# Load order, Ln/Exp order and the place of a q turn at the start of a fused attention and FFN kernel

## The chip, the cores and the metric

The kernel runs on one core of one Trainium2 chip. The metric is device time in microseconds (us) of that core, as the median over executions of the whole kernel. Lower is better. Beside the timed runs there is one execution taken by the hardware profiler; all views quoted below come from it.

## The reference

Two computations follow each other: an attention whose keys and values are first projected from 1024 positions to 64, and a feed-forward layer with three parallel first matrices.

```
k_proj = E @ k ; v_proj = F @ v                 # per batch and head: 1024 -> 64 positions
scores = scale * q @ k_proj.T                   # 1024 x 64
attn   = softmax(scores)                        # max is taken off first, 1e-9 added to the sum
x      = attn @ v_proj                          # heads side by side: 8192 tokens x 512
h      = max(x @ w1, x @ w2, x @ w3)            # 512 -> 768, elementwise maximum of three products
out    = h @ w_out                              # 768 -> 512, float32
```

There are 8 batches of 8 heads, 1024 positions and 64 channels. All inputs are float32 in memory; the kernel works in bf16 with float32 accumulation.

## The kernel before

**Order of work.** The order of every instruction is written out by hand; no scheduler moves anything. Each engine works through its own list in the order in which the program emits it, and waits on semaphores where data, buffers or banks are not ready. The FFN of batch b is the trunk. For each of its two halves (chunks of 512 tokens) the function `l1` runs 18 times: for each of six column blocks jt, once for each of w1, w2 and w3 (i = 0, 1, 2). Each call is four matmuls into one of four rotating PSUM banks (0 to 3). The bank of w1 is copied out by ScalarE into `h1s` (L181), that of w2 is joined with `h1s` by VectorE into `m12` (L183), that of w3 with `m12` into `hT` (L185). `down` (L202, six matmuls over the six blocks of `hT`, copied out by ScalarE at L204) makes the output rows of a quarter chunk; every second one starts a store on POOL's queue (L209).

**Slots.** Between these calls the attention of batch b+1 is slipped in. After each `l1` or `down` a counter `slot` goes up by one in `tick`, and when it reaches the number that stands with a group, that group is emitted. The groups are `kv` (both projections, L117 and L119, then the copies to `kp2` at L123 and L124 and the turn of `kp2` into `kpT`, L166), `scores(0)` and `scores(1)` (four heads each, L136, with the Exp at L139), `sums` (the softmax sums by matmuls with ones, then on ScalarE Ln and Exp for each half u, L153 and L154, which give `rinv` = 1/sum), `av(0)` and `av(1)` (L146, each scaled by `rinv` on VectorE into `xT`, L159). All of them share PSUM banks 4 to 7, so each has to wait until the one before it has been read out.

During batch 0 the slots stand closer. Slots 1 to 12 belong to `l1_first` (L368), 13 to 16 to the first four `down`, 17 to 34 to the 18 calls of `l1` of the second chunk, 35 to 38 to its four `down`. Batch 1's attention sits there at slots 19 (`kv`), 26 and 29 (`scores`), 32 (`sums`), 34 and 36 (`av`); `q_pe1` at 22 and 24 turns batch 1's q on TensorE. From batch 1 on the slots are 2, 10, 15, 20, 25 and 30.

**Loads and turns.** Loads go through POOL's queue, at most eight outstanding in turn, and land in the order of issue. `load(b, ...)` issues two DMAs for q or k and three for v. `load_behind_turn(b)` first lets POOL copy one column of the `kpT` of the batch before (`seen`, L91), so that the loads of batch b are issued only after that turn has landed. q is turned by two transposing DMAs (`q_turn`, L97), one for four heads each, on SyncE's (SP) queue. The turn of `kp2` is on the same queue, so a turn that is emitted later runs behind it. In batch 0 both halves of batch 2's `q_turn` are emitted at slot 28; batch 2's `kv`, with its turn, comes at slot 2 of batch 1.

**Start.** Batch 0's attention runs ahead of everything, by pairs of heads: `k_proj0`, `scores0`, `v_proj0`, `av0`, `norm0`. The first chunk's product with w1 is `w1_ct(ct)` for four slices ct of the inner dimension (six matmuls each, L361). Slice 0 needs heads from the first two pairs alone, slices 2 and 3 need the last two pairs. `warmup` matmuls without use fill gaps.

Of the kernel before, what the change touches and what calls it, by code (L numbers as in the profile page):

```python
# [16 lines left out]
def kernel(ctx: ExitStack, tc: tile.TileContext, q, k, v, E, F, w1, w2, w3, w_out, out):  # L17
    nc = tc.nc
    B, H, S, D = q.shape
    KP = E.shape[0]  # L20
    P = 128
    SI = S // P
# [3 lines left out]
    NPAIR = H // 2  # L26
# [54 lines left out]
    def load(b, src, dst):  # L81
        sv = src[b].rearrange("h (p si) d -> p h si d", si=SI)
        parts = [(slice(0, 4), slice(0, 4)), (slice(4, 8), slice(4, 8))]
        if src is v:
            parts[1:] = [(slice(4, 8, 2), slice(5, 8, 2)), (slice(5, 8, 2), slice(4, 8, 2))]
        for slots, heads in parts:
            nc.gpsimd.dma_start(out=dst[b % NB][:, slots], in_=sv[:, heads])  # L87

    def load_behind_turn(b):

        nc.gpsimd.tensor_copy(out=seen, in_=kpT[(b - 1) % NB][:, 0, 0:1])  # L91
        load(b, q, q_t)
        load(b, k, k_t)
        load(b, v, v_t)

    def q_turn(b, hs):
        nc.sync.dma_start_transpose(  # L97
# [14 lines left out]
    def attention(b, turn):  # L112
        i = b % NB

        def kv():
            for si in range(SI):
                nc.tensor.matmul(out=ps[0:KP, AB, :], lhsT=eT[:, si, :], rhs=k_t[i][:, :, si, :],  # L117
                                 start=(si == 0), stop=(si == SI - 1))
                nc.tensor.matmul(out=ps[KP:P, AB, :], lhsT=fT[:, si, :], rhs=v_t[i][:, :, si, :],  # L119
                                 start=(si == 0), stop=(si == SI - 1))  # L120
            kv_k = ps[0:KP, AB, :].rearrange("p (h d) -> p h d", d=D)
            kv_v = ps[KP:P, AB, :].rearrange("p (g u dd f) -> p u g f dd", u=2, f=2, dd=HD)
            nc.scalar.copy(out=kp2[i][:, :, 0, :], in_=kv_k)  # L123
            nc.vector.tensor_copy(out=kp2[i][:, :, 1, :], in_=kv_k)  # L124
            turn(i)
            nc.scalar.copy(out=vp2[i][KP:P], in_=kv_v[:, 1])
            nc.vector.tensor_copy(out=vp2[i][0:KP], in_=kv_v[:, 0])

        def scores(u):
            for gg in range(2):  # L130
                g = 2 * u + gg
                for par in range(2):
                    r = slice(par * D, (par + 1) * D)
                    for col in range(2):
                        h = HEAD[2 * g + col]
                        nc.tensor.matmul(out=ps[col * KP:(col + 1) * KP, AB + 2 * gg + par, :],  # L136
                                         lhsT=kpT[i][r, h, :], rhs=qT[i][r, h, :, :], start=True, stop=True)
            for gg in range(2):
                nc.scalar.activation(out=pT[:, 2 * u + gg, :, :], in_=ps[:, AB + 2 * gg:AB + 2 * gg + 2, :],  # L139
                                     func=AF.Exp, scale=scale)  # L140

        def quads(lhs):
            for par in range(2):
                for hh, j, g, u in QUADS:
                    rows = slice(u * KP, (u + 1) * KP)
                    nc.tensor.matmul(out=ps[j * HD:(j + 1) * HD, AB + 2 * hh + par, :],  # L146
                                     lhsT=lhs(rows, g), rhs=pT[rows, g, par, :], start=True, stop=True,
                                     tile_position=(u * KP, j * HD))

        def sums():  # L150
            quads(lambda rows, g: ones[rows, :])
            for u in range(2):
                nc.scalar.activation(out=lns[u], in_=ps[:, AB + 2 * u:AB + 2 * u + 2, :], func=AF.Ln)  # L153
                nc.scalar.activation(out=rinv[u], in_=lns[u], func=AF.Exp, scale=-1.0)  # L154

        def av(half):
            quads(lambda rows, g: vp2[i][rows, g, half, :])
            for u in range(2):
                nc.vector.tensor_tensor(out=xT[b % 3][:, 2 * u + half, :, :], in0=ps[:, AB + 2 * u:AB + 2 * u + 2, :],  # L159
                                        in1=rinv[u].rearrange("p (c n) -> p c n", c=2), op=ALU.mult)  # L160

        return [(2, kv), (10, lambda: scores(0)), (15, lambda: scores(1)), (20, sums),
                (25, lambda: av(0)), (30, lambda: av(1))]

# [62 lines left out]
    def v_proj0(g, bank):  # L227
        for si in range(SI):
            for u in range(2):
                nc.tensor.matmul(out=ps[u * KP:(u + 1) * KP, bank, g * D:(g + 1) * D], lhsT=fT[:, si, :],  # L230
                                 rhs=v_t[0][:, HEAD[2 * g + u], si, :], start=(si == 0), stop=(si == SI - 1))
        nc.vector.tensor_copy(out=vp2[0][:, g], in_=ps[:, bank, g * D:(g + 1) * D].rearrange("p (dd f) -> p f dd", f=2))
# [54 lines left out]
    def warmup(n, bank):  # L287
        for _ in range(n):
            nc.tensor.matmul(out=ps[:, bank, :], lhsT=warm[:, 0:P], rhs=warm, start=True, stop=True)
# [8 lines left out]
        (nc.scalar if g % 2 else nc.sync).dma_start(out=q_st[:, 2 * g:2 * g + 2], in_=qv_[0][:, 2 * g:2 * g + 2])  # L298

    make_identity(nc, ident)  # L300
    for src, dst in ((k, k_t), (v, v_t)):
        sv = src[0].rearrange("h (p si) d -> p h si d", si=SI)
        for g in range(NPAIR):
            nc.gpsimd.dma_start(out=dst[0][:, 2 * g:2 * g + 2], in_=sv[:, 2 * g:2 * g + 2])
    wv = w1.rearrange("(hh r f) n -> hh f r n", hh=2, f=2)
    for ct in range(NCT):
        nc.gpsimd.dma_start(out=w_sb[0][:, ct, :], in_=wv[ct // 2, ct % 2])
    for wt, w in zip(w_sb[1:], (w2, w3)):
        for hh in range(2):
            nc.gpsimd.dma_start(out=wt[:, 2 * hh:2 * hh + 2, :],  # L310
                                in_=w[hh * 256:(hh + 1) * 256].rearrange("(r f) n -> r f n", f=2))
# [44 lines left out]

    W1B = (0, 1, 4, 5, 2, 3)

    def w1_ct(ct):
        for jt in range(NJT):  # L360
            nc.tensor.matmul(out=ps[:, W1B[jt], :], lhsT=w_sb[0][:, ct, jt * P:(jt + 1) * P], rhs=xT[0][:, ct, 0, :],  # L361
                             start=(ct == 0), stop=(ct == NCT - 1))

# [24 lines left out]
    av0(1, 0)  # L388
    norm0(0, 0, 6, (0,))
    norm0(0, 1, 7, (0,))  # L390
    for g in (2, 3):
        warmup(1, 2)
        v_proj0(g, 3)
    w1_ct(0)
    av0(0, 1)
    av0(1, 1)
    norm0(0, 0, 5, (1,))
    norm0(0, 1, 6, (1,))
    w1_ct(1)
    w1_ct(2)  # L400
    w1_ct(3)
    for jt in range(NJT):
# [3 lines left out]
    for b in range(B):  # L406
        groups = attention(b + 1, turn_dma) if b + 1 < B else []
        if b == 0:
            g1 = [g for _, g in groups]
            groups = [(10, q_up0), (11, scores_up0), (13, lambda: sums0(1, 4)), (15, av_up0),  # L410
                      (19, g1[0]), (22, lambda: q_pe1(0)), (24, lambda: q_pe1(1)), (26, g1[1]), (29, g1[2]),
                      (32, g1[3]), (34, g1[4]), (36, g1[5])]
        slot = 0
        gi = 0

        def tick():
            nonlocal slot, gi
            slot += 1
            while gi < len(groups) and groups[gi][0] <= slot:
                groups[gi][1]()  # L420
                gi += 1
            if b == 0:
                if slot == 22:
                    load_behind_turn(2)
                if slot == 28:
                    q_turn(2, slice(0, H // 2))
                    q_turn(2, slice(H // 2, H))
            elif b + 2 < B:
                if slot == 9:
                    load_behind_turn(b + 2)  # L430
                if slot == 18:
                    q_turn(b + 2, slice(0, H // 2))
                if slot == 27:
                    q_turn(b + 2, slice(H // 2, H))

        for ch in range(2):
            c = 2 * b + ch
            if c == 0:
                for i, jts, banks in ((1, range(6), (6, 7, 0, 1, 4, 5)), (2, range(3), (2, 3, 6)), (2, range(3, 6), (0, 1, 2))):
                    for _ in l1_first(i, jts, banks):  # L440
                        tick()
                state["f"] = 2
                for tt in range(4):
                    down(0, 0, 0, tt)
                    tick()
                continue
            for s in range(18):
                l1(b, ch, c, s // 3, s % 3)
                tick()
                if pend and s in (2, 5, 8, 11):  # L450
                    pend.pop(0)()
                    tick()
            pend = [lambda tt=tt, b=b, ch=ch, c=c: down(b, ch, c, tt) for tt in range(4)]
        if b == 0:
            while pend:
                pend.pop(0)()
                tick()
# [32 lines left out]
```

## Time and profile before

| | |
|---|---|
| median of 4 runs | 404.54 us (404.11 to 404.72) |
| the profiled execution's own time | 402.63 us |
| its span, first to last instruction | 400.8 us |
| TensorE busy | 392.2 us, 98% of the span |
| VectorE, ScalarE, POOL busy | 185.4, 167.7, 70.8 us |
| chain that ended last | 91% TensorE, 6% DMA, 1% ScalarE, 1% VectorE |

The span is the time from the first to the last instruction; 1.8 us more lie around it in the profiled execution. A busy TensorE is no TensorE at its peak, because its matmuls overlap and their ends are modelled: one matmul of 512 columns shows 379 ns, but 12 in a row take 2.70 us in the chain, about 0.22 us each. The chain is followed back from the last instruction to whatever released each step, so where it leaves TensorE, TensorE may have stood still for some or all of that piece.

### The profile page before, as it was taken

To read this page: it belongs to the slowest core of one execution; us is meant where nothing else is said; L and a number is where in the kernel's file an instruction comes from. 1 tells how busy PE (TensorE), PEld (TensorE's weight loads), DVE (VectorE), ACT (ScalarE), POOL (GpSimd) and SP (SyncE) were. 2 spreads that over 40 slices of the span, in tenths; PEclk is the share of its full clock that TensorE was granted. 3 is DMA by queue.
4 is the path that set the end of the run, shared out by engine and by line. 5 is a ranking of instruction groups with operands and counts; after the bars stand their busy time and mean duration, and the time that the engine had idled before them with its cause. 6 is when DMAs were issued, how large, how long until landed. Compare 5 with 4: busy or idle time off the path is not lost.

```text
span 400.8 us, 5985 instructions
## 1 busy us (share of the span) xinstructions
PE 392.2 (98%) x2422; PEld 170.9 (43%) x2422; DVE 185.4 (46%) x268; ACT 167.7 (42%) x248; POOL 70.8 (18%) x109
## 2 busy tenths in 40 slices
PE   7999999999999999999999999999999999999996
PEld 4444353434444444444444444444444444444443
DVE  3346354554653365533744246433655337433441
ACT  3413467346424553246322663245532473222222
POOL 7351150132001501051000500024010000000000
PEclk9899999999999999999999999999999999999999
DMA  9999969969951999149940899129991211102023
GB/s 227 206 209 206 213 162 194 206 107 189 201 119 52 174 170 195 56 94 184 227 138 13 155 192 232 52 59 171 192 170 57 63 52 50 56 0 106 1 104 107
DMA packets 62651, 53.73 MB, mean 134 GB/s; under 512 B 30496, under 2 KB 57632, under 8 KB 62624
## 3 DMA queue, kind: packets, MB, share of 16 engines
q0 software_dynamic: 31760, 43.52, 53.8%
q1 hardware_dynamic: 30032, 8.92, 15.4%
q10 hardware_dynamic: 832, 0.92, 0.7%
q8 instruction: 19, 0.31, 0.3%
q14 instruction: 8, 0.07, 0.1%
HBM read 57.15 MB, written 16.78 MB: 184 GB/s over the span
## 4 chain that ended last, share of the span: by engine, by line
PE 91%; DMA 6%; ACT 1%; DVE 1%; issue 0%; POOL 0%; POOLq 0%; DVEq 0%
PE ps L178 57%; PE ps L202 20%; PE ps L117 3%; PE ps L146 3%; DMA w_sb<-in_moe_w_dram 3%; PE ps L368 3%; PE ps L136 2%; DMA k_t<-in_k_dram 2%; DMA kpT<-kp 2%; PE ps L361 1%; ACT lns L153 0%; DVE xT L250 0%; PE ps L281 0%; PE ps L195 0%; PE ps L217 0%
## 5 line engine op out<-in xcount | busy, mean ns | idle before, releaser
L178 PE MATMUL ps<-xT,w_sb 128*128 128x512 bf16 x1080 | 246.6, 379 | 0.2 <-DVE xT L250 0.2
L178 PEld LDWEIGHTS <-w_sb 128*128 128x128 bf16 x1080 | 103.2, 98 | 132.7 <-issue 12.8
L183 DVE TENSOR_TENSOR m<-ps,h1s 128x512 f32<-128x512 f32 x90 | 62.1, 690 | 145.3 <-PE ps L178 114.9
L202 PE MATMUL ps<-wo_sb,hT 128*128 128x512 bf16 x378 | 91.2, 379 | 0.0
L181 ACT COPY h1s<-ps 128x512 f32<-128x512 f32 x90 | 52.6, 584 | 68.4 <-PE ps L178 68.0
L204 ACT COPY o_acc<-ps 128x512 f32<-128x512 f32 x63 | 36.8, 585 | 98.5 <-PE ps L202 98.5
L209 POOL DMA_DIRECT2D out_dram<-o_acc x30 | 21.2, 707 | 282.2 <-ACT o_acc L204 282.2
L185 DVE TENSOR_TENSOR hT<-ps,m 128x512 bf16<-128x512 f32 x90 | 62.3, 692 | 12.9 <-PE ps L178 4.8
L202 PEld LDWEIGHTS <-hT 128*128 128x128 bf16 x378 | 35.7, 98 | 47.2 <-issue 6.0
L159 DVE TENSOR_TENSOR xT<-ps,rinv 128x1024 bf16<-128x1024 f32 x28 | 32.9, 1217 | 8.5 <-PE ps L146 8.5
L139 ACT ACTIVATE pT<-ps 128x1024 bf16<-128x1024 f32 x28 | 27.2, 1022 | 12.4 <-PE ps L136 12.4
L87 POOL DMA_DIRECT2D v_t<-in_v_dram x21 | 15.3, 760 | 3.3 <-DMA w_sb<-in_moe_w_dram 3.3
L154 ACT ACTIVATE rinv<-lns 128x1024 f32<-128x1024 f32 x14 | 14.8, 1057 | 0.4
L153 ACT ACTIVATE lns<-ps 128x1024 f32<-128x1024 f32 x14 | 14.2, 1014 | 0.9 <-PE ps L146 0.9
L119 PE MATMUL ps<-v_t,fT 128*64 128x512 bf16 x56 | 13.4, 382 | 0.0
L117 PE MATMUL ps<-k_t,eT 128*64 128x512 bf16 x56 | 13.4, 382 | 0.0
L87 POOL DMA_DIRECT2D q_t<-in_q_dram x14 | 10.6, 764 | 4.4 <-DMA q_t<-in_q_dram 2.0
L368 PE MATMUL ps<-xT,w_sb 128*128 128x512 bf16 x48 | 10.9, 379 | 0.0
L123 ACT CAST kp<-ps 64x512 bf16<-64x512 f32 x7 | 4.0, 578 | 16.0 <-PE ps L119 16.0
L87 POOL DMA_DIRECT2D k_t<-in_k_dram x14 | 10.5, 765 | 0.8 <-issue 0.4
L124 DVE CAST kp<-ps 64x512 bf16<-64x512 f32 x7 | 4.8, 682 | 12.2 <-ACT kp L123 12.2
L146 PE MATMUL ps<-pT,vp 64*32 64x512 bf16 x224 | 9.1, 381 | 1.0 <-ACT lns L153 1.0
(77 smaller groups left out, 141.9 us busy)
## 6 DMA issues: line engine op xcount, KB each, us to landing
out_dram<-o_acc POOLq DMA_DIRECT2D x30, 512.0 KB, 5.1
q_t<-in_q_dram POOLq DMA_DIRECT2D x15, 512.0 KB, 7.8
k_t<-in_k_dram POOLq DMA_DIRECT2D x14, 512.0 KB, 13.0
v_t<-in_v_dram POOLq DMA_DIRECT2D x18, 256.0 KB, 17.7
v_t<-in_v_dram POOLq DMA_DIRECT2D x7, 512.0 KB, 16.7
w_sb<-in_moe_w_dram POOLq DMA_DIRECT2D x4, 384.0 KB, 10.3
k_t<-in_k_dram POOLq DMA_DIRECT2D x4, 256.0 KB, 7.9
w_sb<-in_moe_w_dram POOLq DMA_DIRECT2D x4, 192.0 KB, 10.2
```

The lines of the kernel that those rows point to most:

```text
L87: nc.gpsimd.dma_start(out=dst[b % NB][:, slots], in_=sv[:, heads])
L117: nc.tensor.matmul(out=ps[0:KP, AB, :], lhsT=eT[:, si, :], rhs=k_t[i][:, :, si, :], start=(si == 0), stop=(si == SI - 1))
L139: nc.scalar.activation(out=pT[:, 2 * u + gg, :, :], in_=ps[:, AB + 2 * gg:AB + 2 * gg + 2, :], func=AF.Exp, scale=scale)
L159: nc.vector.tensor_tensor(out=xT[b % 3][:, 2 * u + half, :, :], in0=ps[:, AB + 2 * u:AB + 2 * u + 2, :], in1=rinv[u].rearrange("p (c n) -> ...
L178: nc.tensor.matmul(out=ps[:, bank, :], lhsT=w_sb[i][:, ct, jt * P:(jt + 1) * P], rhs=xT[b % 3][:, ct, ch, :], start=(ct == 0), stop=(ct == ...
L181: nc.scalar.copy(out=h1s[jt % 2], in_=ps[:, bank, :])
L183: nc.vector.tensor_tensor(out=m12[jt % 2], in0=ps[:, bank, :], in1=h1s[jt % 2], op=ALU.max)
L185: nc.vector.tensor_tensor(out=hT[c % 2][:, jt, :], in0=ps[:, bank, :], in1=m12[jt % 2], op=ALU.max)
L202: nc.tensor.matmul(out=ps[:, bank, :], lhsT=hT[c % 2][:, jt, tt * P:(tt + 1) * P], rhs=wo_sb[:, jt, :], start=(jt == 0), stop=(jt == NJT - 1))
L204: nc.scalar.copy(out=o[:, tt, :], in_=ps[:, bank, :])
L209: nc.gpsimd.dma_start(out=dst[:, tt - 1:tt + 1, :], in_=o[:, tt - 1:tt + 1, :])
L368: nc.tensor.matmul(out=ps[:, bank, :], lhsT=w_sb[i][:, ct, jt * P:(jt + 1) * P], rhs=xT[0][:, ct, 0, :], start=(ct == 0), stop=(ct == NCT ...
```

## The change

The diff has four parts.

- **Start.** w1's slice 0 is loaded ahead of batch 0's last v pair instead of behind it. `w1_ct(0)` runs before the last `v_proj0`, which moves from bank 3 to bank 7; one half of `w1_ct(1)` runs ahead of the second `av0`, the other half behind. One `warmup` matmul goes.
- **`sums`.** Both Ln are emitted ahead of both Exp, in every batch.
- **Slots of batch 1's attention in batch 0.** `scores(0)`, `scores(1)` and `sums` come one slot earlier.
- **Batch 2.** It loads k, v, q instead of q, k, v. The first half of its `q_turn` stays at slot 28 of batch 0; the second goes to slot 3 of batch 1, behind the turn of batch 2's `kp2`.

```diff
-    def load_behind_turn(b):
+    def load_behind_turn(b, order="qkv"):
         nc.gpsimd.tensor_copy(out=seen, in_=kpT[(b - 1) % NB][:, 0, 0:1])
-        load(b, q, q_t)
-        load(b, k, k_t)
-        load(b, v, v_t)
+        for c in order:
+            load(b, *{"q": (q, q_t), "k": (k, k_t), "v": (v, v_t)}[c])
...
             for u in range(2):
                 nc.scalar.activation(out=lns[u], in_=ps[:, AB + 2 * u:AB + 2 * u + 2, :], func=AF.Ln)
+            for u in range(2):
                 nc.scalar.activation(out=rinv[u], in_=lns[u], func=AF.Exp, scale=-1.0)
...
+    for g in range(NPAIR):
+        load0(k, k_t, g)
+    for g in range(NPAIR - 1):
+        load0(v, v_t, g)
     for ct in range(NCT):
         nc.gpsimd.dma_start(out=w_sb[0][:, ct, :], in_=wv[ct // 2, ct % 2])
+        if ct == 0:
+            load0(v, v_t, NPAIR - 1)
...
-    for g in (2, 3):
-        warmup(1, 2)
-        v_proj0(g, 3)
+    v_proj0(2, 3)
+    warmup(1, 2)
     w1_ct(0)
+    v_proj0(3, 7)
+    w1_ct(1, range(3))
     av0(0, 1)
     av0(1, 1)
     norm0(0, 0, 5, (1,))
     norm0(0, 1, 6, (1,))
-    w1_ct(1)
+    w1_ct(1, range(3, NJT))
     w1_ct(2)
...
-                      (19, g1[0]), (22, lambda: q_pe1(0)), (24, lambda: q_pe1(1)), (26, g1[1]), (29, g1[2]),
-                      (32, g1[3]), (34, g1[4]), (36, g1[5])]
+                      (19, g1[0]), (22, lambda: q_pe1(0)), (24, lambda: q_pe1(1)), (25, g1[1]), (28, g1[2]),
+                      (31, g1[3]), (34, g1[4]), (36, g1[5])]
...
                 if slot == 22:
-                    load_behind_turn(2)
+                    load_behind_turn(2, "kvq")
                 if slot == 28:
                     q_turn(2, slice(0, H // 2))
-                    q_turn(2, slice(H // 2, H))
-            elif b + 2 < B:
+                return
+            if b == 1 and slot == 3:
+                q_turn(2, slice(H // 2, H))
+            if b + 2 < B:
```

More of the change, by code (lines that the diff above doesn't have):

```diff
@@ L300, with load0 @@
     make_identity(nc, ident)
[L301 to L304, printed above, removed]
     wv = w1.rearrange("(hh r f) n -> hh f r n", hh=2, f=2)
+    def load0(src, dst, g):
+        nc.gpsimd.dma_start(out=dst[0][:, 2 * g:2 * g + 2],
+                            in_=src[0].rearrange("h (p si) d -> p h si d", si=SI)[:, 2 * g:2 * g + 2])
+    for g in range(NPAIR):
+        load0(k, k_t, g)
+    for g in range(NPAIR - 1):
+        load0(v, v_t, g)
     for ct in range(NCT):
         nc.gpsimd.dma_start(out=w_sb[0][:, ct, :], in_=wv[ct // 2, ct % 2])
+        if ct == 0:
+            load0(v, v_t, NPAIR - 1)
     for wt, w in zip(w_sb[1:], (w2, w3)):
@@ L357, with w1_ct @@
     W1B = (0, 1, 4, 5, 2, 3)
-    def w1_ct(ct):
-        for jt in range(NJT):
+    def w1_ct(ct, jts=range(NJT)):
+        for jt in jts:
             nc.tensor.matmul(out=ps[:, W1B[jt], :], lhsT=w_sb[0][:, ct, jt * P:(jt + 1) * P], rhs=xT[0][:, ct, 0, :],
```

## The prediction, made before the changed kernel had run

> **What bounds the kernel now.** I read the page first (shares and chain), then the chain of waits in order of time, TensorE's own waits, the timeline where those waits lie, and the DMA queues by stretch. The page:
>
> ```profile
> PE 392.2 (98%) x2422; PEld 170.9 (43%) x2422; DVE 185.4 (46%) x268; ACT 167.7 (42%) x248; POOL 70.8 (18%) x109
> PE 91%; DMA 6%; ACT 1%; DVE 1%; issue 0%; POOL 0%; POOLq 0%; DVEq 0%
> ```
>
> TensorE sets the end. A change pays only where TensorE stands still, and costs wherever it makes TensorE stand still. The chain in order of time shows where it leaves TensorE:
>
> ```profile
> 8.91 10.70 DMA w_sb<-in_moe_w_dram
> ...
> 19.66 1.47 PE ps L361 x6
> ...
> 65.27 1.02 ACT lns L153
> ...
> 67.37 0.92 ACT lns L153
> ...
> 79.96 6.29 DMA kpT<-kp
> ...
> 86.29 0.63 PE ps L136 x8
> ```
>
> TensorE's waits say how much of these pieces is a real standstill:
>
> ```profile
> PE ps L146 <- ACT lns L153: 1.0, 1, 1.0
> ...
> PE ps L136 <- DMA kpT<-kp: 0.7, 1, 0.7
> ```
>
> So of the 6.29 us of the kpT turn only 0.7 are lost. The first wait is dearer than its 1.0: one L146 starts at 66.95 and the other fifteen at 68.33, 1.38 us lost. The timeline there shows ScalarE's queue:
>
> ```profile
> 64.67 0.58 ACT L181 COPY h1s<-ps 128x512 f32<-128x512 f32 x1 [0.77 <-PE ps L178]
> ...
> 65.26 1.02 ACT L153 ACTIVATE lns<-ps 128x1024 f32<-128x1024 f32 x1
> ...
> 68.31 1.06 ACT L154 ACTIVATE rinv<-lns 128x1024 f32<-128x1024 f32 x1
> ```
>
> Ln, Exp, Ln, Exp follow one another from 65.26 to 69.37, and the copy L181 stands ahead of them. Last, the DMA queues, packets, MB and share, for 66 to 74 us:
>
> ```profile
> q0 software_dynamic: 1246, 1.24, 91.1%
> q1 hardware_dynamic: 1248, 0.32, 30.1%
> ```
>
> and for 200 to 201 us:
>
> ```profile
> q1 hardware_dynamic: 1032, 0.26, 128.1%
> ```
>
> q0 carries the loads, q1 the turns. Beside loads a turn gets 1248/8 = 156 packets per us; alone up to 1032.
>
> **What the Trainium skill says.** "DMA: Bandwidth & Descriptors", Queues, rings and completion order: each DMA engine goes round its queues packet by packet. The 1246 against 1248 packets agree. "TensorE: Matmul & The Clock Gate", Part 1: after an idle window of about 3.4 us TensorE drops to half clock until it has been busy for about as long again. TensorE has no such gap after 20 us and its clock row is all 9s there, so the trace neither confirms nor denies it. The same page, Architectural detail: ScalarE and VectorE are strict FIFO; the timeline above agrees.
>
> **The change, part by part.** Times are those of before unless said.
>
> *Start.* v's last pair lands at 18.6, w1 slice 0 at 19.61 (8.91 + 10.7). They swap: the slice takes about 0.95, so it lands at 17.33 (v's third pair) + 0.95 = 18.3, v's last at 19.6; everything behind keeps its place. `w1_ct(0)` also needs `xT` from L250, ready at 17.66 + 0.65 = 18.3. It starts at 18.4 instead of 19.66, ends at 19.7; `v_proj0(3)` (0.35) till 20.1; slice 1 lands at 20.55 as before, three matmuls till 21.25; `av0` (0.55) till 21.8; the other 15 matmuls (3.3) till 25.1, against 25.66. Gain **0.55**, bounds 0.3 to 0.9. w2's first half landed at 24.3, so the next loads still cover it (w2's second half 26.2 for 27.7). One warmup matmul (0.39 shown) lies in a DMA wait: nothing.
>
> *Ln first, and slots 25, 28, 31.* Everything from `scores(0)` to `sums` comes one `l1` (0.87) earlier. `scores(0)` then follows the q copies on banks 4 and 5 (done at 57.13) at 57.19: no wait. `sums` go from 64.57 to 63.70, Ln from 64.39 to 66.34. `av(0)` comes at 67.05 and waits no longer: 1.3 us won. But `sums` now precedes the sixteenth `l1`, whose copy L181 therefore queues behind Ln, Ln, Exp, Exp (4 x 1.04 less overlaps): 68.17 to 68.75 instead of 64.67. Behind it wait L183 (0.69, till 69.47) and L185 (till 70.27), which writes the last sixth of `hT`. The first `down` needs that sixth at 68.8: TensorE stands 1.5 us. L159 follows in VectorE's queue (70.2 to 72.54), and `av(1)`, at 71.93, waits for it: 0.6 more. `down` three starts at 73.2 instead of 72.14. Loss **1.06**, bounds 0.5 to 1.5. In later batches `sums` has five slots to `av(0)`; the four operations take as long in either order, so nothing behind them moves: zero, and if that cover were gone, 1 us a batch.
>
> *Batch 2's loads and turns.* POOL issues the same seven DMAs at about 55; k and v land by 68 instead of 76.6, q's halves near 71 and 74. SP issues turn a at 71; it lands near 79 with the two stores between. Let K be the start of batch 2's `kv` (76.6 before). kpT's turn is issued at K+3.3 (79.96) with nothing ahead, and lands after 2.6 (as at 122.3), K+5.9, where `scores(0)` wants it at K+9.0: the 0.68 us wait goes. Gain **0.68**, bounds 0.4 to 0.7.
>
> SP issues turn b behind it, at K+4.5 (kpT's issue takes 1.20). What is late next is this turn. `scores(1)` needs it at 91.34 - 0.68, K+14.0. Six first halves show about 3.9 us from issue to first packet (60.92 to 64.9); kpT's quarter-sized turn 1.2, loaded or not, so I take 3.9 as its own work: K+8.4. Meanwhile kpT's earlier landing frees `seen` and batch 3's loads: POOL issues q 0.67 after the landing (86.25 to 86.92), K+6.6, against K+10.3 before, and they flow fully 2.8 us later (89.7), **K+9.4**. So turn b has 1.0 us nearly alone and then shares. kpT's 128 KB took 544 packets, so half of q's turn is 4 x 512 + 32 = 2080. Alone: 560 per us (kpT's pace) to 1030, I take 750, as first load packets already trickle. From K+9.4 to K+14.0: 4.6 x 156 = 720. Missing 610, at 156 per us 3.9, with 0.2 for the landing **4.1 us** of standing TensorE. Ends: 330 missing, 2.1; 800 missing, 5.1; with no free stretch at all 2080/156 = 13.3, landing at K+21.7, 7.7. A stop over 3.4 us may add half-clock time, 0 to 1.7 (half of 3.4); I take 0.
>
> Sum: -0.55 + 1.06 - 0.68 + 4.1 = +3.9. The profiled execution took 402.63 (span 400.8 and 1.8 around it), 1.9 below the median; the difference is put on the median: **408.5**. About 0.2%, 0.8 us, can be told from no change.
>
> **The rivals.**
> - *A, forecast:* turn b is caught by batch 3's loads. Own range 406.5 to 412.
> - *B, turn b slips through:* if its first packets come by about K+7.5 (a wait of 3.0 rather than 3.9), or the loads flow 0.8 later, it is done before K+14 and the sum is -0.17: 404.4 (403.8 to 405). For it: everything hangs on under 1 us, and no trace shows such a turn issued on idle queues. Against: kpT's 1.2 is the same loaded or idle. Not slower, from that point.
> - *C, all three waits go and nothing takes their place:* B, and the late copy L181 hidden: -0.55 - 1.38 - 0.68, 401.9. It needs the last sixth of `hT` by 68.8, against which the written order of ScalarE speaks.
> - *D, no free stretch and half clock after it:* 7.7 + 1.7 in place of 4.1, 413.8.
> - *The change does not do what it says:* the order of instructions of the built program shows every move on POOL, SP, ScalarE and TensorE, so no.
>
> **The numbers.** A 0.66, B 0.18, C 0.10, D 0.06. Slower: A, D and a little of B, 0.74; same: most of B, 0.12; faster: C and some of B, 0.14. Range 403.8 to 412.5; C and D stay outside, 0.16.
>
> **What would show it.** In the profile after: `w1_ct(0)` near 18.4; L146 of `av(0)` without a wait on Ln, but L202 waiting for L185 near 70; no wait of L136 on kpT; and L136 waiting 2 to 5 us for the qT turn, with batch 3's loads issued some 3 us earlier and turn b taking 12 us or more to land. The forecast is wrong if turn b lands within 9.5 us of its issue, or if TensorE never waits on qT.

## The result, and the profile after

The changed kernel takes 402.88 us in the median (402.01 to 404.51, 44 runs) against 404.58 us (401.83 to 407.23, 63 runs) for the kernel before. The ratio over all runs, not of the two medians, is 0.9965, 95% interval 0.9952 to 0.9977: 1.4 us faster, 0.9 to 1.9. The forecast was 408.5, slower, with a range of 403.8 to 412.5. Three runs of before, at 407.81, 408.08 and 408.25 us, count as slow, being over 1.5% above its fastest, and are left out of the ratios and spreads further down. The profiled execution of the changed kernel took 402.66 us (span 400.7), no less than the profiled one of before (402.63). So the two traces do not show the gain between them; the experiments further down say why.

The page of the changed kernel, engines and chain:

```profile
PE 392.4 (98%) x2421; PEld 170.5 (43%) x2421; DVE 185.7 (46%) x268; ACT 166.2 (41%) x248; POOL 70.9 (18%) x109
PE 94%; ACT 2%; DVE 2%; DMA 1%; issue 1%; DVEq 0%
```

DMA has fallen from 6% of the chain to 1%, ScalarE and VectorE have taken some of its place. TensorE's own waits (who waited for whom: total, times, longest). Line numbers are those of each kernel; L145 and L152 of the changed one are L146 and L153 of before:

```profile
PE ps L202 <- DVE hT L185: 1.5, 1, 1.5
...
PE ps L145 <- DVE xT L159: 0.3, 1, 0.3
```

The waits on Ln (1.0) and on kpT (0.7) are gone. Two new ones stand in their stretch, both foretold: `down` waits for the last sixth of `hT`, and `av(1)` for `xT`. No line has TensorE waiting on a qT turn. The timeline around the new wait:

```profile
64.26 1.94 ACT L152 ACTIVATE lns<-ps 128x1024 f32<-128x1024 f32 x2 [1.06 <-PE ps L145]
...
66.09 2.00 ACT L154 ACTIVATE rinv<-lns 128x1024 f32<-128x1024 f32 x2
...
67.98 0.58 ACT L181 COPY h1s<-ps 128x512 f32<-128x512 f32 x1
68.60 0.69 DVE L183 TENSOR_TENSOR m<-ps,h1s 128x512 f32<-128x512 f32 x1 [3.88 <-ACT h1s L181]
69.39 0.69 DVE L185 TENSOR_TENSOR hT<-ps,m 128x512 bf16<-128x512 f32 x1
...
70.14 1.68 PE L202 MATMUL ps<-wo_sb,hT 128*128 128x512 bf16 x7 [1.51 <-DVE hT L185]
```

Read it downwards: the copy L181 comes behind two Ln and two Exp, VectorE waits 3.88 us for it, and TensorE waits 1.51 us for VectorE. Last, SP's queue in the stretch the forecast turned on. The first two lines give start and duration of an issue; the last two are turn b's own (duration of its issue in ns, its start, its time to landing):

```profile
71.72 2.76 SPq L96 DMA_TRANSPOSE qT<-q_t  x1
80.68 1.20 SPq L166 DMA_TRANSPOSE kpT<-kp  x1
...
L96 SPq DMA_TRANSPOSE qT<-q_t x1: 2037/2037/2037, 82.0 to 82.0; - x1
...
DMA to landing us min/median/max: 5.0/5.0/5.0
```

Turn b is issued at 81.97 and lands at 86.96. `scores(1)` comes at 91.2. It was never near being late.

### The profile page after: what moved, and what is told of

It reads as the page before. It is cut to its first block, busy times and chain, and to the rows that moved or that the text cites. A ratio compares the mean times of both kernels' runs of the same rounds, so it can differ in the third digit from the quotient of the medians.

```text
span 400.7 us, 5984 instructions
## 1 busy us (share of the span) xinstructions
PE 392.4 (98%) x2421; PEld 170.5 (43%) x2421; DVE 185.7 (46%) x268; ACT 166.2 (41%) x248; POOL 70.9 (18%) x109
## 4 chain that ended last, share of the span: by engine, by line
PE 94%; ACT 2%; DVE 2%; DMA 1%; issue 1%; DVEq 0%
PE ps L178 58%; PE ps L202 20%; PE ps L116 3%; PE ps L145 3%; PE ps L375 3%; PE ps L135 2%; PE ps L368 1%; DMA v_t<-in_E_dram 1%; DVE xT L250 1%; PE ps L237 1%; PE ps L223 1%; DVE xT L159 1%; PE ps L327 1%; PE ps L333 1%; PE ps L217 1%
## 5 line engine op out<-in xcount | busy, mean ns | idle before, releaser
L181 ACT COPY h1s<-ps 128x512 f32<-128x512 f32 x90 | 52.8, 587 | 65.4 <-PE ps L178 65.1
L185 DVE TENSOR_TENSOR hT<-ps,m 128x512 bf16<-128x512 f32 x90 | 62.3, 692 | 13.7 <-PE ps L178 5.7
L159 DVE TENSOR_TENSOR xT<-ps,rinv 128x1024 bf16<-128x1024 f32 x28 | 32.9, 1217 | 7.8 <-PE ps L145 7.8
L152 ACT ACTIVATE lns<-ps 128x1024 f32<-128x1024 f32 x14 | 13.6, 1021 | 1.9 <-PE ps L145 1.9
L145 PE MATMUL ps<-pT,vp 64*32 64x512 bf16 x224 | 9.1, 381 | 0.3 <-DVE xT L159 0.3
```

Of the source, the lines that this page charges most:

```text
L181: nc.scalar.copy(out=h1s[jt % 2], in_=ps[:, bank, :])
L185: nc.vector.tensor_tensor(out=hT[c % 2][:, jt, :], in0=ps[:, bank, :], in1=m12[jt % 2], op=ALU.max)
```

## The experiments

Three lengths taken from every profile separate the parts of the change, whatever the total does (all in us): from the first matmul of batch 0's softmax sums to the first with w2 (start), from batch 1's `kv` to batch 2's (Ln and slots), and from batch 2's `kv` to batch 3's (batch 2's loads and turns).

| kernel | start | kv 1 to kv 2 | kv 2 to kv 3 |
|---|---|---|---|
| before, first profile | 10.86 | 28.28 | 42.40 |
| changed | 10.07 | 29.22 | 41.53 |
| batch 2 part alone | 10.70 | 28.28 | 41.52 |
| start part alone | 10.07 | 28.28 | 41.57 |
| Ln and slots alone | 10.70 | 29.23 | 41.68 |
| changed, old slots | 10.07 | 27.28 | 41.52 |
| before, five more profiles | 10.71, 10.70, 10.71, 11.25, 10.70 | 28.28 in each | 41.52, 42.97, 45.54, 41.52, 43.15 |

**Batch 2 part alone.** Before, plus:

```diff
-                    load_behind_turn(2)
+                    load_behind_turn(2, "kvq")
...
-                    q_turn(2, slice(H // 2, H))
...
+            if b == 1 and slot == 3:
+                q_turn(2, slice(H // 2, H))
```

> The kernel before with the batch 2 part alone (k, v, q order; second half of the q turn behind the turn of kp2). Theory 1, the spread of before (401.8 to 407.2) comes from the crowded queues around batch 2, whose cost differs between executions and which this part removes: faster than before by 1.5 to 3 us in the median, and a spread of under 2.5 us. Theory 2, the spread lies elsewhere (start or clock) and this part removes only the 0.7 us wait that the profile of before shows: faster by 0.5 to 0.8 us, spread as before. In the profile, by both: turn b issued near 81 with its first packets about 1.2 us later, landed by 87, and no wait of TensorE on it.

Measured: 403.33 us against 404.09, ratio 0.9992 (0.9968 to 1.0016); its 14 runs spread over 2.5 us (401.62 to 404.14), those of before over 6.0 (401.52 to 407.48). Turn b was issued at 82.5 and landed at 87.5, with no wait on it. The total cannot tell theory 1 from 2. The narrower spread speaks for theory 1; the profiles below decide it.

**Start part alone.** Before, with only the first part of the diff.

> The kernel before with the start part alone. By the sum of the prediction faster by 0.55 us (0.3 to 0.9). Theory 1 (spread sits at batch 2): the spread stays at some 5 us. Theory 2 (spread sits in the start, where the granted clock is still low for a varying time): a gain over 1 us and a smaller spread.

Measured: 403.25 us, ratio 0.9994 (0.9973 to 1.0015), runs from 401.88 to 407.79. The spread stays, as theory 1 has it. Inside the profile the start is 10.70 - 10.07 = 0.63 us shorter, close to the forecast's 0.55; the total is too noisy to show 0.6.

**Ln and slots alone.** Before, plus Ln ahead of Exp and:

```diff
-(26, g1[1]), (29, g1[2]), (32, g1[3])
+(25, g1[1]), (28, g1[2]), (31, g1[3])
```

> The kernel before with both Ln ahead of both Exp and scores(0), scores(1), sums of batch 1 one slot earlier, nothing else. By the sum of the prediction slower by 1.06 us (0.5 to 1.5): L202 waits about 1.5 us for L185 near 70 us, and av(1) some 0.3 to 0.6 for L159. Rival: the loss is taken up again by slack behind it (batch 2 loads and turns have 1 us more time), then the difference is 0 to 0.4 us.

Measured: 404.03 us, ratio 0.9998 (0.9978 to 1.0018). By the changed kernel's line numbers, the profile has the wait on L185 (1.5) and that on L159 (0.3), and kv 1 to kv 2 grows by 29.23 - 28.28 = 0.95. The loss is there, but the total does not show it. The next stretch is 41.68, only 0.16 above one without a wait, and the runs spread over 3.0 us (402.25 to 405.26) where those of before spread over 6.0. That fits the rival: `kv` comes 0.95 us later, batch 2's turns do not, so less of the wait on kpT is left. One profile does not prove it.

**The changed kernel with the old slots.** Ln stays first, the slots go back:

```diff
-(25, g1[1]), (28, g1[2]), (31, g1[3])
+(26, g1[1]), (29, g1[2]), (32, g1[3])
```

> The changed kernel with the old slots 26, 29, 32 for batch 1's scores and sums, Ln still first. If the copy L181 behind Ln, Ln, Exp, Exp is what costs 2.1 us there (1.06 lost against before, and 1.03 that Ln first would have won), this is faster than the changed kernel by about 2 us, so about 401 us, and L202 no longer waits for L185. Rival: the time is bound elsewhere by then (batch 2's turn b, which comes 2 us nearer to its need): the gain is under 0.5 us and L135 waits on the turn.

Measured: **401.23 us** (400.12 to 402.44), ratio 0.9940 (0.9919 to 0.9960). This is faster than before, and its median lies 1.65 us below that of the changed kernel. Its timeline shows the copy ahead again:

```profile
64.98 0.59 ACT L181 COPY h1s<-ps 128x512 f32<-128x512 f32 x1 [0.77 <-PE ps L178]
65.56 1.94 ACT L152 ACTIVATE lns<-ps 128x1024 f32<-128x1024 f32 x2
67.38 2.00 ACT L154 ACTIVATE rinv<-lns 128x1024 f32<-128x1024 f32 x2
```

kv 1 to kv 2 is 27.28: 1.94 below the changed kernel and 1.00 below before. Ln first is worth 1.0 us by itself; the three earlier slots turned that into a loss of 0.94. They were moved together; that the slot of `sums` is the one that costs is read from the timeline.

**Turn b beside batch 3's loads.** The kernel just shown, with batch 3's loads let go before the turn:

```diff
-                if slot == 9:
-                    load_behind_turn(b + 2)
+                if slot == (1 if b == 1 else 9):
+                    load_behind_turn(b + 2, behind=b != 1)
```

With `behind` false the copy to `seen` is left out.

> The changed kernel with the old slots 26, 29, 32, and batch 3's loads not held behind batch 2's kpT turn (the copy to seen is left out for batch 3 alone and the loads are issued at slot 1 of batch 1), so that they flow from about 80 us, before turn b is issued. This brings about what the forecast assumed. If the 3.9 us to the first packet and the 156 packets per us come from loads that run beside the turn: kpT's turn takes 5 to 6 us in place of 2.6, turn b shows no own packet for 3.5 to 4 us, lands 14 to 18 us after its issue, and TensorE waits on it 4 to 8 us: 405 to 409 us. Rival, a turn's pace is its own and loads matter little: turn b lands within 7 us and the time stays near 401 us.

Measured: 414.94 us (413.89 to 415.4), ratio 1.0261 (1.0204 to 1.0318), 13.7 us above the kernel it was made from. TensorE's waits:

```profile
PE ps L136 <- DMA qT<-q_t: 6.4, 1, 6.4
PE ps L136 <- DMA kpT<-kp: 3.5, 1, 3.5
```

kpT's turn took 9.1 us instead of 2.6. Turn b, behind it on the same queue until 88.29, took 20.4 instead of 5.0. Between 81 and 84 us, that is up to 3 us after turn b's issue, the queues moved (packets, MB, share):

```profile
q0 software_dynamic: 498, 0.49, 110.7%
q1 hardware_dynamic: 20, 0.01, 1.3%
```

Twenty packets of turns, the first at 83.45: kpT's turn, issued at 79.20, had waited 4.25 us for it. Once turns and loads flow together they share packet by packet, at the 156 per us of the forecast (86 to 96 us):

```profile
q0 software_dynamic: 1562, 1.55, 91.5%
q1 hardware_dynamic: 1567, 0.39, 30.2%
```

So the mechanism of the forecast exists, and is dearer than expected here; it needs loads that are already under way when the turn is issued. In this profile kv 2 to kv 3 is 55.81, 14.3 more than 41.52, and the two waits make 9.9 of that. After the stops the clock is lower, too: the columns are stretch, us, busy time of TensorE, its weight loads, VectorE, ScalarE and POOL, granted clock, DMA share, GB/s.

```profile
89.00:100.00 11.00, 6.07 (x20) 2.15 (x18) 2.77 (x4) 2.31 (x3) 0.00 (x0) 0.84 1.22 196
100.00:110.00 10.00, 8.56 (x46) 2.96 (x47) 2.08 (x3) 3.42 (x5) 0.00 (x0) 0.66 0.60 100
```

**Order or place.** Two kernels do one half of the batch 2 part each. The first loads k, v, q and leaves both halves of the turn at slot 28; the second loads q, k, v and moves the second half to slot 3 of batch 1.

> The kernel before with batch 2 loading k, v, q, but both halves of its q turn left at slot 28, ahead of the kpT turn. Theory 1a, the order of the loads is what counts: as fast as the batch 2 part alone (403.3 median). Theory 1b, the place of the second half counts: turn b is issued near 75 and lands near 82 with the stores beside it, kpT's turn behind it lands some 1 us later than in the batch 2 part alone but still ahead of scores(0): same time within 0.4 us. If kpT's turn is caught, L136 waits 0.5 to 2 us.

> The kernel before with the second half of batch 2's q turn behind the kpT turn, but q still loaded first. v is still the last to land (near 77, when kv wants it). Theory a, the load order matters: kpT's turn now stands behind the first half alone, which lands near 78, so the wait of L136 on kpT goes (41.5 us from kv to kv) and only a wait of L119 on v of up to 0.5 us stays. Turn b is issued near 81 on emptying queues and lands by 87. Theory b, the first half, which runs beside the loads, is caught by them and holds up kpT's turn: L136 waits 0.5 us or more.

Measured: 403.04 us, ratio 0.9970 (0.9953 to 0.9987), and 403.0 us, ratio 0.9975 (0.9953 to 0.9997). In both profiles kv 2 to kv 3 is 41.52 to 41.53, with no wait on kpT or v. Either half is enough: in the first the second half lands at 84.74 and kpT's turn right behind it at 84.92, 2.6 us before `scores(0)` at 87.56; in the second kpT's turn has only the first half ahead of it (landed at 76.73). Theory a of the second holds as far as kpT goes; the wait on v that it allowed for did not come.

**The kernel before, five more profiles.** The same program each time.

> The kernel before again, for another profile: its own times spread from 401.5 to 408.3 us, and the profile used for the prediction was one of the short ones (402.63). Theory 1: a longer execution (over 404) has waits of TensorE near batch 2 that the first profile lacks, L119 on batch 2's v or L136 on the kpT or qT turns, together 1 to 4 us. Theory 2: it has only a longer start, 1 to 2 us later at the first L361 with a lower granted clock, and the same waits behind it. If it is again a short one (under 403), the same waits as before.

> The kernel before a third time, for one more profile of another execution. Expectations as for the second: theory 1, waits of 1 to 4 us on batch 2's loads or turns in a long execution; theory 2, only a later start.

> The kernel before a fourth time. So far three profiles lost 0.9, 0.0 and 1.45 us between batch 2's kv and batch 3's (42.40, 41.52, 42.97 us against 41.52 with batch 2 loading k, v, q). Theory 1: this loss goes on to 2 to 4 us in the longest executions (405 to 408), and it alone makes them long. Theory 2: it never passes 1.5 us, and the rest of the spread is the start (first w1 matmul between 19.7 and 21.8 us) and the half-clock windows.

> The kernel before a fifth time, as the fourth: the stretch from batch 2's kv to batch 3's is 41.5 plus the wait on the kpT turn (0 to 1.5 us by theory 2, more in a long execution by theory 1).

> The kernel before a sixth time, as the fourth and fifth: theory 1, over 2 us lost at batch 2 if it is longer than 405 us; theory 2, at most 1.5 us and a late start.

Measured, total and loss between kv 2 and kv 3 against 41.52: 402.27 and 0.0; 404.20 and 1.45; 406.61 and 4.02; 401.82 and 0.0; 403.94 and 1.63; with the first profile's 402.63 and 0.88 the mean loss is 1.33 us. The third of these is a long execution. Its wait on kpT and its chain:

```profile
PE ps L136 <- DMA kpT<-kp: 1.9, 1, 1.9
...
81.11 7.49 DMA kpT<-kp
88.60 0.04 issue
88.64 0.63 PE ps L136 x8
89.27 6.11 PE ps L178 x20
```

kpT's turn stands behind both halves of q's turn (the second landed at 88.36). `scores(0)` is reached 11.19 us after `kv` instead of 8.86 where nothing waits, 2.3 us lost. Then twenty matmuls take 6.11 us where they take 4.42 in the first profile. The stretches around them, columns as above:

```profile
86.00:89.30 3.30, 1.42 (x13) 0.40 (x12) 0.63 (x1) 0.78 (x2) 0.22 (x2) 1.00 0.63 168
89.30:92.80 3.50, 3.50 (x9) 1.22 (x9) 0.76 (x2) 1.74 (x2) 3.37 (x5) 0.51 0.53 85
92.80:96.00 3.20, 3.20 (x21) 1.24 (x20) 1.90 (x3) 0.82 (x2) 1.76 (x3) 1.00 1.15 181
```

TensorE is busy for 1.42 of 3.3 us, and in the next 3.5 us it is granted half the clock: 1.7 us more. Theory 1 holds for the loss. It is not alone in the spread: the first matmul with w1 comes between 19.66 and 20.76 us in these six profiles, and theory 2's late start accounts for that much. The two together are all of it: take from each span the time of the first matmul with w2 and the loss (404.80 - 26.40 - 4.02 in the long one), and 374.4 is left in all six, alike within 0.02 us. The late start goes with the clock: between 12.5 and 13.5 us the granted clock is 1.00 in the two with w1 at 19.66 and 19.82, and 0.50 in the four with w1 at 20.28 to 20.76. That the one makes the other was not tried.

## Why the prediction was wrong

*Start, -0.55.* Right: 10.07 in all four profiles that have the new start, 10.70 or 10.71 in seven with the old one, so 0.63. Three more with the old start have 10.48, 10.86 and 11.25; in the last two TensorE came early and waited for the loads.

*Ln and slots, +1.06.* Right, by its mechanism and nearly in size: +0.94. The wait on L185 was to be 1.5 us and is 1.51; the wait of `av(1)` was to be 0.6 and is 0.25 in the timeline. Taken apart, Ln first gives -1.00 (the old slots), where the prediction had 1.3, and the earlier slots +1.94. "In later batches nothing moves" held: kv to kv there is the same in all kernels.

*The kpT wait, -0.68.* Right mechanism, wrong size. The term was read off one profiled execution. Six executions lose 0.0 to 4.02 us there, 1.33 on average, and the five profiles with k, v, q or the split turn, batch 3's loads held back, lose none (41.52 or 41.53). With this mean the parts sum to -0.63 + 0.94 - 1.33 = -1.0 us, against a gain of 1.4 measured (0.9 to 1.9). The six profiled executions average 403.6 us, the medians of before lie at 404.1 to 404.7, so 1.33 is probably too low. The forecast did put its difference on a median that lay 1.9 us above the profile, without asking what the longer executions spent the 1.9 on.

*Turn b, +4.1: the step that failed.* "kpT's quarter-sized turn 1.2, loaded or not, so I take 3.9 as its own work." In the changed kernel the first half, issued at 71.72, has its first packet at 72.90, 1.2 us later, as a quarter-sized turn does; its issue takes 2.76 us and turn b's 2.04, not 7.4 and more; turn b lands 5.0 us after its start. The 3.9 us was time behind loads. All six turns from which it was taken had been issued into running loads, because each waits for the very load that others follow. The kpT turn that seemed to show the same pace under load was issued at 51.56, when batch 1's last load was landing (51.64) and only two stores were left; with loads still queued it waits 4.25 us for its first packet. So turn b was not caught at K+8.4 with a window of 1.0 us; with the same 1.2 us its packets run from about K+5.8 on (K is 77.37 in the changed kernel). Batch 3's loads were issued from 84.32 on, but between 82 and 86 us they moved almost nothing:

```profile
q1 hardware_dynamic: 2547, 0.64, 89.2%
q0 software_dynamic: 3, 0.00, 0.5%
```

Turn b landed at 86.96, 4 us ahead of `scores(1)`. Both signs that the prediction named for being wrong are there: a landing within 9.5 us of the issue, and no wait of TensorE on qT. Rival B named this point, first packets by K+7.5, and is what happened. It was given 0.18, and its own sum, -0.17, lay too high mostly by the kpT term. Rival C's 401.9 is off by less than the forecast, but not for its reason: the late copy L181 was not hidden. The kernel with the old slots, 401.23, is the case that C describes.

Which loads make the 3.9 is not settled. The first half of the changed kernel's q turn, too, was issued while a load was in full flow: between 71.7 and 72.8 us, ahead of its first packet, the queues moved

```profile
q0 software_dynamic: 217, 0.22, 119.1%
```

But that was the last load, landing at 74.19. The six turns with 3.9 had five or more loads still to land. How many it takes was not tried.

*Clock.* Taken as 0 beside a range of 0 to 1.7 for a stop of over 3.4 us. In the changed kernel the clock did not fall; in the kernel before it is part of the loss (1.7 us in one of six executions), and it is a part of the 14.3 where the loads were let go early.

What stays open besides: why a single order of instructions loses 0 in one execution and 4.0 in the next. The second q turn lands at 84.2, 84.6, 86.0, 87.4, 87.6 and 88.4 in the six, and the wait on kpT follows it; what makes the transfers differ was not tried.

## What to carry to other kernels

A duration read from transfers that always ran in a crowd is a price of the crowd: before it is used for a quiet place, look for one that ran alone, and if there is none, keep both ends and let neither be the likeliest. Where single executions differ by more than the change is worth, one profile prices one execution; take lengths between two fixed points from several profiles, which here repeat to 0.01 us where nothing waits while the totals differ by 5 us. A step moved one slot earlier takes its whole queue with it: ask which copy now comes behind it.

## What the runs showed of the hardware

- A transposing DMA of 512 KB took 5.0 us from issue to landing with no loads flowing (turn b of the changed kernel), and 17.1 to 19.8 beside loads (the six first halves of before). A quarter-sized one took 2.6, and 9.1 beside loads.
- The first packet of such a DMA came 1.2 to 1.6 us after its issue with at most one load left to land, and 3.9 to 4.4 us after it with five or more.
- A queue of small packets gets its share in packets, not in bytes: 1567 packets of turns against 1562 of loads in 10 us were 0.39 MB against 1.55 (loads let go early).
- A stop of TensorE of 1.9 us was followed by 3.5 us at a granted clock of 0.51 (the long execution of before). "TensorE: Matmul & The Clock Gate" of the Trainium skill, Part 1, puts the limit at an idle window of about 3.4 us; here less was enough, once. Stops of 1.4 and 1.2 us in two other executions of the same kernel left the clock as it was.
